# Cosine attention and a GELU feed-forward on one core: the first w_in tile takes the place of three idle matmuls, and VectorE alone sums a quad of heads in PSUM

## The chip, the cores and the metric

One core of a Trainium2 chip runs the whole program. The metric is the device time of one execution in microseconds.

## The reference

```python
q_n = q / (norm(q) + 1e-6); k_n = k / (norm(k) + 1e-6)        # q, k, v: 8 x 12 x 448 x 64, fp32
attn = softmax(q_n @ k_n.T / tau)                             # tau = 0.1
x = (attn @ v), heads side by side                            # 3584 x 768
out = gelu_exact(x @ w_in) @ w_out                            # 768 -> 2048 -> 768, fp32 result
```

## The kernel before

There are eight batches of 12 heads and 448 positions. A *quad* is four heads; a batch has three (quads 0 to 23 in all). The order of every engine's instructions is written out by hand: the program's text is the order, each engine runs its own queue in that order, and semaphores are derived from who writes and reads which tile.

**A quad.** `load_qk` brings q and k in (SP's queue). `square` (GpSimd, in the first batch ScalarE) and `reduce` (VectorE) make the squared norms `nq`; `logs` and `roots` (ScalarE: ln, then exp of half of it) and `inverses` (VectorE) make the inverse norms `rn`; `scale` (GpSimd) writes the normalised bf16 `qkb`. `transposes` turns it into `qkT`, by a transposing DMA on SP's queue or, for the first quads and quad 3, by TensorE through a PSUM bank `tp` (`copies` on VectorE takes it out). `scores` writes `st` for two of the heads' rows at a time into a pair of PSUM banks; `exps` (ScalarE) turns it into `pt`; there are seven chunks. The sum over the keys is made in one of two ways: by TensorE with a matrix of ones (`sums`, then `turned` and `inverted`), or by adding the seven `pt` chunks into `acc` (`folded` on GpSimd, `chunked` on VectorE) and then across partitions on VectorE (`turned_all`, `inverted_all`). `values` writes `o` into PSUM, `spread` and `normalise` (VectorE) write the batch's `x`.

**The feed-forward.** `first(b)` makes 16 tiles `hp` (m = 0 to 15) of x @ w_in, each of six steps kd, and their gelu `g` on ScalarE. Steps 0 and 1 need quad 0 of the batch, 2 and 3 quad 1, 4 and 5 quad 2; the weights `wi` are loaded by steps, too (`load_wi`, GpSimd's queue). The first tiles (`ahead`) do steps 0 to 3, then 4 and 5 when the last quad's x is there; the rest go tile by tile. In batches 0 and 1 ScalarE swaps its table after the gelu of tile 5, makes the norms of a coming quad, and swaps back. The second matmul (`op`, 16 steps each) is cut into single matmuls and spread as filler over the next batch's attention.

**PSUM.** Eight banks: two singles `mm0` and `mm1` that `mm_tile` hands out in turn (to `op`, `sm`, `tp`, and `hp` tiles), pairs `st0` and `st1`, and a third pair that serves `sm` and `o` in the first batch and is `st2` afterwards. In `first(b)`, `pairs` says which tiles `hp` take which pair: `{0: 1, 2: 0, 6: 1, 8: 0}` means that tiles 0 and 1 take pair 1, 2 and 3 pair 0, and so on; the others take singles.

**Around the change.** In the first batch, `spin(3)` (L453) issues three matmuls whose result nobody reads; it stands in `attention_first` behind the last scores and exponentials of quad 2 and ahead of that quad's last sums. In batch 0 the two TensorE transpositions of quad 3 stand ahead of tile m = 8:

```python
            if b == 0 and m == 8:
                for i in range(2):
                    transposes(4, i)
                    copies(4, i)
```

In batches 2 to 6, `first(b)` also sums the next batch's first quad: `chunked` reduces its first half over the seven chunks in one VectorE instruction (L268), and `folded` adds the second half chunk by chunk on GpSimd (L264).

Of the kernel before, what the change touches and what calls it, by code (L numbers as in the profile page):

```python
# [9 lines left out]
F32 = mybir.dt.float32  # L10
BF16 = mybir.dt.bfloat16
AF = mybir.ActivationFunctionType
ALU = mybir.AluOpType
# [3 lines left out]
def kernel(  # L17
# [17 lines left out]
    nc = tc.nc  # L35
    B, H, S, D = q.shape
    C = S // D
    NQ = H // 4
# [3 lines left out]
    KD = d_model // 128  # L42
    KF = d_ff // 128
    NH = d_model // 2
    NB = S // 32
# [12 lines left out]
    accp = ctx.enter_context(tc.tile_pool(name="accp", bufs=1))  # L58
# [6 lines left out]
    acc = ctx.enter_context(ExitStack())  # L65
# [27 lines left out]
    wi = wpool.tile([128, KD, d_ff], BF16, tag="wi")  # L93
# [7 lines left out]
    def mm_tile(name, shape=(128, 512), dtype=F32, aside=None):  # L101
        t = ps_mm.tile(list(shape), dtype, tag=f"mm{turn[0] if aside is None else turn[0] ^ aside}", name=name)
        if aside is None:
            turn[0] ^= 1
        return t

    def pair(i, name):
        pool = third[0] if i == 2 else ps_st
        return pool.tile([128, 2, 512], F32, tag=f"st{i}", name=name)
# [13 lines left out]
    x_t, g_t = {}, {}  # L123
# [37 lines left out]
    def reduce(u, part=slice(0, 2)):  # L161
        g, s0, s1 = units[u]
        sq = sq_t[g][:, :, s0:s1]
        n, j = place[u]
        if n not in nq_t:
            nq_t[n] = nrm.tile([128, len(groups[n]), 2, s1 - s0, C], F32, tag="nq", name=f"nq{n}")
        nq = nq_t[n][:, j]
        nc.vector.tensor_reduce(nq[:, part], sq[:, part], mybir.AxisListType.X, ALU.add)  # L168
# [54 lines left out]
    def copies(u, i):  # L223
        g, s0, s1 = units[u]
        rows = slice(64 * s0, 64 * s1)
        nc.vector.tensor_copy(qkT_t[g][rows, i], tp_t.pop((u, i))[rows])

    st_t, all_t = {}, {}
# [26 lines left out]

    acc_t = {}

    def folded(g, chunks=range(C), s=slice(0, 2)):
        for c in chunks:
            if c == 1 and g not in acc_t:  # L260
                acc_t[g] = accp.tile([128, 2, S], F32, tag="acc", name=f"acc{g}")
            if c:
                to = acc_t[g][:, s]
                nc.gpsimd.tensor_tensor(to, all_t[g][:, 0, s] if c == 1 else to, all_t[g][:, c, s], ALU.add)  # L264

    def chunked(g, s):
        acc_t[g] = accp.tile([128, 2, S], F32, tag="acc", name=f"acc{g}")
        nc.vector.tensor_reduce(acc_t[g][:, s], all_t[g][:, :, s].rearrange("p c q -> p q c"),  # L268
                                mybir.AxisListType.X, ALU.add)

    def turned_all(g):
        tr = rcp.tile([128, 2 * NB, 32], F32, tag="tr", name=f"ta{g}")
        nc.vector.transpose(tr.rearrange("p b r -> p (b r)"), acc_t.pop(g).rearrange("p s q -> p (s q)"))  # L273
        su = bank_t[g, "su"] = rcp.tile([128, 2, 2, NB], F32, tag="sa", name=f"sa{g}")
        nc.vector.tensor_reduce(su[:, 0].rearrange("p s b -> p (s b)"), tr, mybir.AxisListType.X, ALU.add)
        for j in range(4):
            o = j ^ 1
            nc.vector.tensor_reduce(su[32 * j:32 * (j + 1), 1].rearrange("p s b -> p (s b)"),
                                    su[32 * o:32 * (o + 1), 0].rearrange("p s (b n) -> p (s b) n", n=1),
                                    mybir.AxisListType.X, ALU.add)  # L280

    def inverted_all(g):
        su = bank_t.pop((g, "su"))
        s2 = rcp.tile([128, 2, NB], F32, tag="su", name=f"su{g}")
        for s in range(2):
            for h in range(2):
                nc.vector.tensor_reduce(s2[64 * s:64 * (s + 1), h],
                                        su[64 * h:64 * (h + 1), :, s].rearrange("p k b -> p b k"),
                                        mybir.AxisListType.X, ALU.add)
        rc = bank_t[g, "rc"] = rcp.tile([128, 2, NB], F32, tag="rc", name=f"rc{g}")  # L290
        nc.vector.reciprocal(rc, s2)
# [152 lines left out]
    def upto(f, n, last=None):  # L444
        last = {load_qk: NG, load_v: NV, root: len(groups), load_wi: NQ + 1, load_wo: 4}.get(f, NU)
        while done.get(f, 0) < min(n, last):
            done[f] = done.get(f, 0) + 1
            f(done[f] - 1)

    def spin(n):  # L450
        ps = ps_mm.tile([128, 512], F32, tag=f"mm{turn[0]}", name="spin")
        for _ in range(n):
            nc.tensor.matmul(ps[:, :S], lhsT=ident, rhs=blank, start=True, stop=True)  # L453

    def attention_first():
        x_t[0] = xp.tile([128, KD, S], BF16, tag="x", name="x0")
        DV, AC, GP = nc.vector, nc.scalar, nc.gpsimd
# [154 lines left out]
        scores(2, ((0, 6), (1, 6)))  # L612
        exps(2, ((0, 6), (1, 6)))
        reduce(4, Q)
        spin(3)
        sums(2, range(3, 7))
        values(2, (4,))
        logs(4)
# [169 lines left out]
    def first(b):  # L788
        sb, hf = divmod(b, 2)
        if hf == 0:  # L790
            g_t[sb] = gp.tile([128, KF, 2 * S], BF16, tag="g", name=f"g{sb}")
        nc.scalar.preload_act_table_set(GELU_SET)
        u = (b + 1) * NQ + 1
        hps = {}
        pairs = ({0: 1, 2: 0, 6: 1, 8: 0}, {2: 0, 4: 1, 6: 2, 8: 0}, {2: 2, 4: 1, 6: 0})[min(b, 2)]
        ahead = 6 if b else 5

        def mm(m, kds):
            for kd in kds:
                nc.tensor.matmul(hps[m], lhsT=wi[:, kd, m * 128:(m + 1) * 128],  # L800
                                 rhs=x_t[b][:, kd, :], start=(kd == 0), stop=(kd == KD - 1))

        def bank(m):
            if m in pairs:
                st = pair(pairs[m], f"hp{b}_{m}")
                hps[m], hps[m + 1] = st[:, 0, :S], st[:, 1, :S]
            elif m not in hps:
                hps[m] = mm_tile(f"hp{b}_{m}")[:, :S]

        for m in (0, 2, 3, 4, 5, 1) if b > 1 else range(ahead):  # L810
            bank(m)
            mm(m, range(KD - 2))
        if b == 0:
            upto(square, u + 3)
            upto(scale, u + 1)
            upto(transposes, u + 1)
            upto(load_wo, 4)
            upto(reduce, u + 3)
        else:
            late = int(b == 1)  # L820
            if b == 1:
                upto(scale, u + 1)
                upto(transposes, u + 1)
            for n in range(2, 4) if b > 1 else ():
                upto(scale, u + n)
                upto(transposes, u + n)
                upto(load_qk, (b + 1) * NQ + 6)
            upto(load_qk, (b + 1) * NQ + 5)
            upto(square, u + 3 if b == 1 else u + 4)
            if 1 < b < B - 1:  # L830
                chunked((b + 1) * NQ, 0)
                folded((b + 1) * NQ, s=slice(1, 2))
                upto(square, u + 6)
                upto(reduce, u + 4)
            upto(reduce, u + 4 - 2 * late)
            if 1 < b < B - 1:
                turned_all((b + 1) * NQ)
                inverted_all((b + 1) * NQ)
                spread((b + 1) * NQ, 0)
                spread((b + 1) * NQ, 1)  # L840
        for kds in ((KD - 2,), (KD - 1,)) if b > 1 else (range(KD - 2, KD),):
            for m in range(ahead):
                mm(m, kds)
        for m in range(KF):
# [4 lines that stand above are left out]
            if m >= ahead and (m == 0 or m - 1 not in pairs):  # L849
                for k in range(m, m + 1 + (m in pairs)):  # L850
                    bank(k)
                    mm(k, range(KD))
            nc.scalar.activation(g_t[sb][:, m, hf * S:(hf + 1) * S], hps.pop(m), AF.Gelu)  # L853
            if b <= 1 and m == 5:
                nc.scalar.preload_act_table_set(EXP_SET)
                upto(root, 6 if b == 0 else 8)
                nc.scalar.preload_act_table_set(GELU_SET)
                upto(scale, u + 2)
                upto(transposes, u + 2)
                if b == 0:  # L860
                    upto(load_qk, 2 * NQ + 1)
                else:
                    upto(square, u + 4)
                    upto(reduce, u + 4)
        if b + 1 < B:
            nc.scalar.preload_act_table_set(EXP_SET)
            if b <= 1:
                visit(b + 1, (0, 1, 2))
            upto(root, 2 * b + 6 + (b > 0))
# [63 lines left out]
```

## Time and profile before

| | |
|---|---|
| median of 3 runs | 406.95 us (406.7 to 408.2) |
| the profiled execution | 407.06 us, its span 405.3 us |
| TensorE busy | 398.9 us, 98% of the span |
| ScalarE, VectorE, GpSimd busy | 247.3, 239.0, 250.0 us |
| span of batch 0's w_in stage | 32.03 to 51.08 us |
| batch 3's w_in stage | starts at 176.2 us |

Engines are PE (TensorE matmul), PEld (its weight loads), DVE (VectorE), ACT (ScalarE), POOL (GpSimd) and SP (a queue of DMA issues). L800 is line 800 of the kernel before. `out<-in` names tiles of the program. Matmuls overlap, so the time that one costs is the distance from start to start and not its duration.

### The profile page before, as it was taken

The page shows a single profiled execution, that of the slowest core. Times are in us where ns is not written, and L with a number is a line of the kernel's source. Part 1 is how long each engine was busy: PE and PEld are TensorE (multiplying, and loading weights), DVE is VectorE, ACT ScalarE, POOL GpSimd, SP SyncE. Part 2 cuts the span into 40 slices and gives each one's busy share as a digit, 9 for nine tenths or more (in the row PEclk, how much of TensorE's full clock was granted, in tenths as well). Part 3 has the DMA queues.
Part 4 walks back from the last instruction along what each step waited for, and adds up shares of the span by engine and source line. Part 5 has one row for each costly group of instructions (what it writes and reads, how often), then busy time and mean ns, then how long its engine had stood idle before and what let it go on. Part 6 is the DMA issues. An engine that isn't in the chain of part 4 may idle for free.

```text
span 405.3 us, 8074 instructions
## 1 busy us (share of the span) xinstructions
PE 398.9 (98%) x3343; PEld 207.9 (51%) x3343; DVE 239.0 (59%) x438; ACT 247.3 (61%) x360; POOL 250.0 (62%) x160
## 2 busy tenths in 40 slices
PE   7999999999999999999999999999999999999996
PEld 3445545455555555555555555555555555455554
DVE  5787214953377976677656976758665981360021
ACT  6995686567867558656566557865656555724300
POOL 5899707075799993999829994799919940000000
PEclk9999999999999999999999999999999999999999
DMA  8999999836395714668083942769032840130033
GB/s 288 261 257 217 204 212 322 184 83 194 69 278 114 186 36 101 206 116 175 10 217 119 197 94 15 254 102 226 0 87 59 155 64 2 40 78 2 0 79 78
DMA packets 66484, 54.52 MB, mean 135 GB/s; under 512 B 38672, under 2 KB 62352, under 8 KB 66448
## 3 DMA queue, kind: packets, MB, share of 16 engines
q1 hardware_dynamic: 54464, 41.79, 40.3%
q0 software_dynamic: 11600, 11.80, 18.2%
q8 instruction: 26, 0.43, 0.4%
q10 hardware_dynamic: 384, 0.43, 0.3%
q14 instruction: 10, 0.08, 0.1%
HBM read 45.61 MB, written 11.01 MB: 140 GB/s over the span
## 4 chain that ended last, share of the span: by engine, by line
PE 91%; DMA 3%; POOL 2%; DVE 2%; issue 1%; ACT 0%; POOLq 0%
PE op L396 34%; PE hp L800 32%; PE st L242 10%; PE o L325 8%; DMA qkT<-qkb 3%; PE spin L453 2%; PE sm L311 2%; PE op L415 1%; POOL qkb L204 1%; PE sm L302 1%; POOL sq L159 1%; PE tp L221 1%; DVE nq L168 1%; DVE rn L188 0%; ACT pt L252 0%
## 5 line engine op out<-in xcount | busy, mean ns | idle before, releaser
L252 ACT ACTIVATE pt<-st 128x896 bf16<-128x896 f32 x168 | 143.1, 916 | 54.0 <-PE st L242 53.7
L396 PE MATMUL op<-wo,g 128*128 128x384 bf16 x864 | 148.9, 327 | 0.0
L800 PE MATMUL hp<-x,wi 128*128 128x448 bf16 x768 | 146.9, 353 | 0.0
L396 PEld LDWEIGHTS <-g 128*128 128x128 bf16 x864 | 81.0, 98 | 64.6 <-issue 13.9
L800 PEld LDWEIGHTS <-wi 128*128 128x128 bf16 x768 | 74.4, 98 | 71.4 <-issue 2.9
L853 ACT ACTIVATE g<-hp 128x448 bf16<-128x448 f32 x128 | 64.1, 549 | 74.0 <-PE hp L800 73.8
L204 POOL TENSOR_TENSOR qkb<-qk,rn 128x896 bf16<-128x896 f32 (+1 forms) x50 | 80.1, 1630 | 27.4 <-DVE rn L188 27.1
L400 DVE COPY ot<-op 128x384 f32<-128x384 f32 x54 | 29.3, 542 | 79.2 <-PE op L396 77.1
L264 POOL TENSOR_TENSOR acc<-acc,pt 128x896 f32<-128x896 f32 (+1 forms) x50 | 73.0, 1460 | 4.2 <-ACT pt L252 0.5
L159 POOL TENSOR_TENSOR sq<-qk 128x1792 f32<-128x1792 f32 (+1 forms) x22 | 66.5, 3038 | 14.1 <-DMA qk<-in_k_dram 14.1
L168 DVE TENSOR_REDUCE nq<-sq 128x28 f32<-128x1792 f32 (+2 forms) x30 | 48.6, 1632 | 10.3 <-POOL sq L159 7.3
L242 PE MATMUL st<-qkT 64*64 64x448 bf16 x672 | 49.5, 358 | 0.8 <-DMA qkT<-qkb 0.6
L325 PE MATMUL o<-pt,v 64*64 64x448 bf16 x672 | 37.0, 351 | 0.0
L359 DVE TENSOR_TENSOR x<-o,rs 128x448 bf16<-128x448 f32 x48 | 28.0, 610 | 13.7 <-PE o L325 12.7
L264 POOL TENSOR_TENSOR acc<-pt 128x896 f32<-128x896 bf16 (+1 forms) x10 | 14.5, 1453 | 28.6 <-ACT pt L252 28.6
L242 PEld LDWEIGHTS <-qkT 64*64 64x64 bf16 x672 | 16.8, 105 | 24.7 <-issue 18.1
L354 DVE STREAM_TRANSPOSE rs<-rc 128x448 f32<-128x448 f32 x48 | 28.6, 625 | 0.7
L268 DVE TENSOR_REDUCE acc<-pt 128x448 f32<-128x3136 bf16 x5 | 28.0, 5603 | 0.0
L325 PEld LDWEIGHTS <-v 64*64 64x64 bf16 x672 | 18.7, 107 | 14.4 <-issue 4.4
L273 DVE STREAM_TRANSPOSE ta<-acc 128x896 f32<-128x896 f32 x10 | 11.1, 1112 | 18.0 <-POOL acc L264 18.0
L333 DVE STREAM_TRANSPOSE tr<-sm 128x448 f32<-128x448 f32 x14 | 9.1, 648 | 15.1 <-PE sm L311 12.8
L186 DVE TENSOR_REDUCE se<-root 128x28 f32<-128x56 f32 (+2 forms) x18 | 4.0, 222 | 15.5 <-ACT root L180 15.3
(48 smaller groups left out, 171.1 us busy)
## 6 DMA issues: line engine op xcount, KB each, us to landing
qk<-in_q_dram SPq DMA_DIRECT2D x23, 448.0 KB, 5.3
qk<-in_k_dram SPq DMA_DIRECT2D x23, 448.0 KB, 5.8
out_dram<-ot SPq DMA_DIRECT2D x48, 192.0 KB, 3.2
v<-in_v_dram POOLq DMA_DIRECT2D x7, 672.0 KB, 6.9
wo<-in_moe_w_out_dram POOLq DMA_DIRECT2D x4, 768.0 KB, 13.9
wi<-in_moe_w_in_dram POOLq DMA_DIRECT2D x4, 512.0 KB, 14.2
out_dram<-ot SPq DMA_DIRECT2D x12, 96.0 KB, 2.2
wi<-in_moe_w_in_dram POOLq DMA_DIRECT2D x4, 256.0 KB, 14.1
```

The lines of the kernel that those rows point to most:

```text
L159: eng.tensor_tensor(sq[:, part], t[:, part], t[:, part], ALU.mult)
L168: nc.vector.tensor_reduce(nq[:, part], sq[:, part], mybir.AxisListType.X, ALU.add)
L204: eng.tensor_tensor(qkb[:, i, :, s0:s1].rearrange("p c s d -> p s c d"), t[:, i, s0:s1], rn[:, i].to_broadcast([128, s1 - s0, C, D]), ALU. ...
L242: nc.tensor.matmul(st[cols, n, :S], lhsT=qkT[rows, 1, c, cols], rhs=qkT[rows, 0, :, cols], start=True, stop=True, tile_position=(64 * s, 6 ...
L252: nc.scalar.activation(pt, st[:, :, :S], AF.Exp, scale=inv_tau)
L264: nc.gpsimd.tensor_tensor(to, all_t[g][:, 0, s] if c == 1 else to, all_t[g][:, c, s], ALU.add)
L325: nc.tensor.matmul(bank_t[g, h][cols, :S], lhsT=v_t[g][rows, s, c, :], rhs=pt_t[g, s, c][rows], start=(c == 0), stop=(c == C - 1), tile_po ...
L354: nc.vector.transpose(rs, bank_t[g, "rc"][:, h].to_broadcast([128, NB, 32]))
L396: nc.tensor.matmul(ps[:, :NH], lhsT=g_t[sb][:, kf, t * 128:(t + 1) * 128], rhs=wo[:, kf, ni * NH:(ni + 1) * NH], start=(kf == 0), stop=(kf ...
L400: nc.vector.tensor_copy(ot[:, ni * NH:(ni + 1) * NH], ps[:, :NH])
L800: nc.tensor.matmul(hps[m], lhsT=wi[:, kd, m * 128:(m + 1) * 128], rhs=x_t[b][:, kd, :], start=(kd == 0), stop=(kd == KD - 1))
L853: nc.scalar.activation(g_t[sb][:, m, hf * S:(hf + 1) * S], hps.pop(m), AF.Gelu)
```

## The change

Batch 0: the three spins are taken out. In their place stand steps 0 to 3 of tile 0 of w_in, in the single bank that the spins wrote. The later tiles take other banks: pair 1 for tiles 1-2 and 7-8, pair 0 for 3-4 and 9-10, singles for the rest. The transpositions of quad 3 still stand at m = 8, but tile 8 is then already done, as it shares a pair with tile 7.

Batches 2 to 6: the next batch's first quad is summed by VectorE alone, both halves at once, seven instructions of 128x896, into bank pair 0 in PSUM. The three squares of that stage now follow one another on GpSimd. `turned_all` transposes the accumulator in two pieces, everywhere. Batches 2 to 7: tiles 6 and 7 of w_in take single banks instead of pair 0, and tiles 8 and 9 pair 2 instead of singles.

```diff
-    def folded(g, chunks=range(C), s=slice(0, 2)):
+    def folded(g, chunks=range(C)):
         for c in chunks:
-            if c == 1 and g not in acc_t:
+            if c == 1:
                 acc_t[g] = accp.tile([128, 2, S], F32, tag="acc", name=f"acc{g}")
             if c:
-                to = acc_t[g][:, s]
-                nc.gpsimd.tensor_tensor(to, all_t[g][:, 0, s] if c == 1 else to, all_t[g][:, c, s], ALU.add)
-
-    def chunked(g, s):
-        acc_t[g] = accp.tile([128, 2, S], F32, tag="acc", name=f"acc{g}")
-        nc.vector.tensor_reduce(acc_t[g][:, s], all_t[g][:, :, s].rearrange("p c q -> p q c"),
+                nc.gpsimd.tensor_tensor(acc_t[g], all_t[g][:, 0] if c == 1 else acc_t[g], all_t[g][:, c], ALU.add)
+
+    def gathered(g, p):
+        acc_t[g] = pair(p, f"acc{g}")[:, :, :S]
+        nc.vector.tensor_reduce(acc_t[g], all_t[g][:, 0].rearrange("p s (q n) -> p s q n", n=1),
                                 mybir.AxisListType.X, ALU.add)
+        for c in range(1, C):
+            nc.vector.tensor_tensor(acc_t[g], acc_t[g], all_t[g][:, c], ALU.add)
 
     def turned_all(g):
         tr = rcp.tile([128, 2 * NB, 32], F32, tag="tr", name=f"ta{g}")
-        nc.vector.transpose(tr.rearrange("p b r -> p (b r)"), acc_t.pop(g).rearrange("p s q -> p (s q)"))
+        acc = acc_t.pop(g)
+        for s in range(2):
+            nc.vector.transpose(tr[:, s * NB:(s + 1) * NB].rearrange("p b r -> p (b r)"), acc[:, s])
...
+    early = {}
+
+    def w_in(b, t, m, kds):
+        for kd in kds:
+            nc.tensor.matmul(t, lhsT=wi[:, kd, m * 128:(m + 1) * 128], rhs=x_t[b][:, kd, :],
+                             start=(kd == 0), stop=(kd == KD - 1))
...
         reduce(4, Q)
-        spin(3)
+        early[0] = mm_tile("hp0_0")[:, :S]
+        w_in(0, early[0], 0, range(KD - 2))
         sums(2, range(3, 7))
...
-        hps = {}
-        pairs = ({0: 1, 2: 0, 6: 1, 8: 0}, {2: 0, 4: 1, 6: 2, 8: 0}, {2: 2, 4: 1, 6: 0})[min(b, 2)]
+        hps = {0: early[0]} if b == 0 else {}
+        pairs = ({1: 1, 3: 0, 7: 1, 9: 0}, {2: 0, 4: 1, 6: 2, 8: 0}, {2: 2, 4: 1, 8: 2})[min(b, 2)]
...
-        for m in (0, 2, 3, 4, 5, 1) if b > 1 else range(ahead):
+        for m in (0, 2, 3, 4, 5, 1) if b > 1 else range(b == 0, ahead):
...
-            upto(square, u + 3 if b == 1 else u + 4)
+            upto(square, u + 3 if b == 1 else u + 6)
             if 1 < b < B - 1:
-                chunked((b + 1) * NQ, 0)
-                folded((b + 1) * NQ, s=slice(1, 2))
-                upto(square, u + 6)
+                gathered((b + 1) * NQ, 0)
                 upto(reduce, u + 4)
```

More of the change, by code (lines that the diff above doesn't have):

```diff
@@ L793, in first @@
         u = (b + 1) * NQ + 1
-        hps = {}
-        pairs = ({0: 1, 2: 0, 6: 1, 8: 0}, {2: 0, 4: 1, 6: 2, 8: 0}, {2: 2, 4: 1, 6: 0})[min(b, 2)]
+        hps = {0: early[0]} if b == 0 else {}
+        pairs = ({1: 1, 3: 0, 7: 1, 9: 0}, {2: 0, 4: 1, 6: 2, 8: 0}, {2: 2, 4: 1, 8: 2})[min(b, 2)]
         ahead = 6 if b else 5
         def mm(m, kds):
-            for kd in kds:
-                nc.tensor.matmul(hps[m], lhsT=wi[:, kd, m * 128:(m + 1) * 128],
-                                 rhs=x_t[b][:, kd, :], start=(kd == 0), stop=(kd == KD - 1))
+            w_in(b, hps[m], m, kds)
         def bank(m):
```

## The prediction

> **What bounds the kernel now.** I read the page first, then the table of waits, then TensorE's timeline around the first batch's w_in stage, then ScalarE's and the load issues of the same stretch.
>
> ```profile
> PE 398.9 (98%) x3343; PEld 207.9 (51%) x3343; DVE 239.0 (59%) x438; ACT 247.3 (61%) x360; POOL 250.0 (62%) x160
> ...
> PEclk9999999999999999999999999999999999999999
> ```
>
> The table of waits (who waited for whom: us in total, times, longest) has, after the start-up, one row of a matmul's wait above 0.2 us:
>
> ```profile
> PE st L242 <- DMA qkT<-qkb: 0.6, 1, 0.6
> ```
>
> So the matrix engine sets the time. From 59.7 us to the end no matmul starts late; taking work from VectorE or GpSimd there can gain nothing, and a change gains only if it removes matmuls, and loses wherever it makes TensorE wait. TensorE's timeline from 26 to 62 us (start, duration, operation, count, idle before):
>
> ```profile
> 29.79 0.74 PE L453 MATMUL spin<-blank,ident 128*128 128x448 bf16 x3
> 30.46 0.95 PE L302 MATMUL sm<-pt,ones 128*64 128x448 bf16 x8
> 31.34 0.76 PE L325 MATMUL o<-pt,v 64*64 64x448 bf16 x12
> 32.03 9.25 PE L800 MATMUL hp<-x,wi 128*128 128x448 bf16 x48
> 41.12 0.94 PE L221 MATMUL tp<-ident,qkb 128*128 128x128 bf16 x14
> 41.90 9.24 PE L800 MATMUL hp<-x,wi 128*128 128x448 bf16 x48
> 51.08 0.76 PE L242 MATMUL st<-qkT 64*64 64x448 bf16 x12
> ...
> 58.16 0.38 PE L242 MATMUL st<-qkT 64*64 64x448 bf16 x4
> 59.16 0.57 PE L242 MATMUL st<-qkT 64*64 64x448 bf16 x8 [0.62 <-DMA qkT<-qkb]
> ```
>
> A w_in step costs (41.12 - 32.03) / 48 = 0.189 us from start to start, a spin the same. Four st matmuls cost 0.19 (x4, x8 and x12 last 0.38, 0.57, 0.76), so the next were due at 58.35 and came at 59.16: 0.81 us lost. That is the only slack of this engine after the start, and anything late before 59 us is forgiven up to 0.81 us.
>
> ScalarE in the same stretch, and GpSimd's and the load queue's answer for the second w_in load:
>
> ```profile
> 36.78 2.81 ACT L853 ACTIVATE g<-hp 128x448 bf16<-128x448 f32 x6 [3.65 <-PE hp L800]
> 39.61 1.28 ACT L855 ACT_TABLE_LOAD   x1
> 41.59 0.34 ACT L175 ACTIVATE lq<-nq,tiny 128x56 f32<-128x56 f32 x1 [0.70 <-DVE nq L168]
> 41.97 0.25 ACT L180 ACTIVATE root<-lq 128x56 f32<-128x56 f32 x1
> 42.24 1.28 ACT L857 ACT_TABLE_LOAD   x1
> 43.53 2.52 ACT L853 ACTIVATE g<-hp 128x448 bf16<-128x448 f32 x5
> ```
>
> ```profile
> 12.07 1.21 POOL L431 DMA_DIRECT2D wi<-in_moe_w_in_dram  x2
> ```
>
> ```profile
> wi<-in_moe_w_in_dram POOLq DMA_DIRECT2D x1, 512.0 KB, 18.8
> ```
>
> After the sixth gelu ScalarE swaps tables, waits for the norms (41.59) and swaps back: no gelu runs from 39.6 to 43.53. The second of the two loads issued from 12.07 starts at 12.7 and takes 18.8 us, so the weights of steps 2 and 3 are complete at 31.5 us. Before, the first matmul that needs them is at 32.03 + 0.38 = 32.4, safe by 0.9 us.
>
> **Part 1: tile 0 in place of three spins.** Removed: three spins, 3 x 0.189 = -0.57 us of TensorE. The four first steps of tile 0 are moved, not added.
>
> First new wait. The moved steps stand at 29.79. Their inputs x (batch 0, quads 0 and 1) are there: the last of these normalisations ends at 29.2. Step 2 would start at 29.79 + 2 x 0.19 = 30.17, where it needs weights that land at 31.5. With a weight load (98 ns in its rows) and the release it starts at about 31.65: a stall of 1.48 us. Behind it in TensorE's queue stand the last sums (30.46) and values of quad 2. After two steps and the 0.28 us that lay between third spin and sums, the sums start at 32.12 instead of 30.46: everything behind them is 1.66 us late. VectorE's turning of these sums (31.45, on the chain of waits) waits for them, and behind it in its queue stand the scales of the next quad. From there the chain of waits runs without slack: rn 32.56, GpSimd qkb 33.05, sq 36.34, VectorE nq 39.54, ScalarE lq 41.59, root, table, gelu at 43.53. So the seventh gelu moves from 43.53 to 45.19 and ends at 45.73 (0.54 each). GpSimd's later issues (two w_out loads at 39.46) and SP's queue (the transposing DMA at 46.50, the q and k loads behind it) move by the same 1.66.
>
> Second new wait. One tile now sits in a single bank ahead of the pairs, so the pairs hold tiles 1-2, 3-4, 7-8, 9-10; tile 5 takes the other single bank and tile 6 the first again. The two transpositions tp of quad 3 come after tile 8 instead of tile 7, and take the single banks of tiles 5 and 6. Before they took those of tiles 4 and 5, both read before the table swap. Now the second must wait for tile 6's gelu, the first one behind the swap. TensorE reaches it thus: 32.03 + 1.66 = 33.69; 16 + 10 + 24 = 50 steps, 9.46 us, to 43.15 (x of quad 2 ends at 35.06 + 1.66 = 36.7, just when step 4 wants it); the first seven transpositions 0.39 (half of 41.12 to 41.90), to 43.54. The gelu ends at 45.73, plus 0.05 for the release: the second seven start at 45.78, a stall of 2.24 us. Then 0.39 and 42 steps at 9.18 / 48: the scores that stood at 51.08 come at 54.2, 3.1 us late.
>
> What is late next. The scores of 58.35 come at 61.5. Their DMA, issued 1.66 later, lands at 59.12 + 1.66 = 60.8: in time, so the old 0.81 us is swallowed. Sum for part 1: -0.57 + 1.48 + 2.24 - 0.81 = **+2.3 us**. Later nothing gives it back: TensorE has no other wait.
>
> **Part 2: VectorE adds the quad alone (batches 2 to 6).** Removed: five VectorE reductions and thirty GpSimd adds. Added: five times seven instructions of 128x896 on VectorE. Rows:
>
> ```profile
> L268 DVE TENSOR_REDUCE acc<-pt 128x448 f32<-128x3136 bf16 x5 | 28.0, 5603 | 0.0
> L264 POOL TENSOR_TENSOR acc<-acc,pt 128x448 f32<-128x448 f32 x25 | 25.8, 1034 | 2.0
> L273 DVE STREAM_TRANSPOSE ta<-acc 128x896 f32<-128x896 f32 x10 | 11.1, 1112 | 18.0 <-POOL acc L264 18.0
> ```
>
> No row shows the new add. The nearest VectorE rows for 896 elements are the turning, 1.11, and its reduction, 1.09; bounds are 0.61 (x, 128x448, a PSUM operand) and 1.89 (GpSimd's add of this size). At 1.13 with the gap between dependent instructions: 7.9 us instead of 5.6. In batch 3 it starts at 181.15 and ends at 189.1; the reduce behind it (2.0) and the turning (now two of 0.63) follow without the 2.63 us wait for GpSimd, and the chain ends at about 196.5 against 196.7 now. The next scale waits for ScalarE's root at 197.0 anyway. The sums now sit in bank pair 0, which the next quad's values (198.1) need: read out by 192.3, 5.8 us ahead. Price taken: 0. At 1.89 per add the chain would end near 201.7, 2 us behind its x at 199.66, in five batches. GpSimd's 6.2 us per batch go, but nothing on TensorE waits for them: 0.
>
> Tile 6 of batches 2 to 7 moves from the free pair into tile 0's bank. Batch 3: the first gelu runs 182.27 to 182.82, the 37th matmul starts at 183.02, 0.20 us later; a matmul that waits for ScalarE starts 0.05 after it here (58.10 to 58.16). Taken 0; bounds 0 and, at half a gelu late, 0.3 x 6 = 1.6 us. The accumulator turned in two pieces adds 0.1 to VectorE, with 0.6 us spare before x is used (181.24 against 181.89).
>
> **A rule against the change.** The page's clock row is full throughout, and the 0.81 us pause at 58 us did not lower it. Only the first spins are slow: 0.373 us apart until 7 us, 0.189 after.
> The Trainium skill, "TensorE: Matmul & The Clock Gate", Part 1, says that TensorE falls to half clock after an idle window of about 3.4 us and needs as long to recover. By it, stalls of 1.5 and 2.2 us cost nothing more; no row here shows a pause of that length.
>
> **Sum.** The profiled execution took 407.06 (span 405.3 and 1.8 around it), 0.1 over the median 406.95 of the runs; +2.3 gives 409.4 and 409.25. I say 409.3. About 0.5% (2.0 us) is what a measurement of this kernel can tell from no change; the sum is just beyond.
>
> **The rivals.**
> Weights in time (not slower): the second w_in load is done by 30.17. Then stall one is gone, the shift is the one extra matmul, 0.19, stall two stays 2.24: -0.57 + 2.24 - 0.81 = +0.9, 407.9. Between, each 0.1 us earlier saves 0.1; below a landing at 31.2 the result is under the bound. For it: loads vary between executions. Against: eight w_in loads took 9.9 to 18.8 us and queue in order.
> The change does what it says: no new wait, -0.57, and the pause at 59.16 takes that back: 407.0. It needs the seventh gelu ahead of the swap; ScalarE's order says no.
> The clock falls in a stall: as at the start, some 14 matmuls at 0.373 for 0.189, +2.6 us: 411.9.
> VectorE or tile 6 late after all: 1.6 us or more on top, from 411.
>
> **How the numbers follow.** Both stalls 0.60 (408.6 to 410; three quarters of it beyond the bound), weights in time 0.14, no new wait 0.08, clock 0.09, VectorE or tile 6 0.07, faster for a reason I do not see 0.02. Slower: 0.45 + 0.09 + 0.07 = 0.61; faster 0.02; the rest 0.37. The range 407.4 to 411.2 holds the first two cases and part of the others.
>
> **What the profile after would show.** Right: a wait of TensorE for DMA wi of about 1.4 us at 30.2; a wait of the tp matmuls for a gelu of about 2.2 us; no wait for qkT at 61; no new TensorE waits from 130 us on; VectorE adds near 1.1 us. Wrong: no wi wait, TensorE waiting at w_in's seventh tile in batches 2 to 7, or for the turning ta at the values; a clock row below 9.

## The result, and the profile after

| | before | after |
|---|---|---|
| median of 16 runs, us | 406.83 | 410.7 |
| ratio (95% interval) | | 1.0073 (1.0046 to 1.0101) |
| profiled execution, span | 407.06, 405.3 | 411.04, 409.3 |

The kernel is slower, by 0.5 to 1.0%. Its runs form two groups: seven at 409.04 to 409.45 us with a mean TensorE clock of 0.998 to 1.0, and eight at 410.68 to 411.61 with 0.994 to 0.996. (One more, at 414.24 with 0.983, belongs to a disturbance that the kernel before shows too, at 412.56 to 414.25 with 0.983; here and below, runs with a mean clock under 0.993 are left out of such counts.) The profiled execution is of the second group.

The page after: TensorE is as busy as before, and the clock row has one dip, in the fifth slice.

```profile
PE 399.6 (98%) x3340; PEld 207.7 (51%) x3340; DVE 250.2 (61%) x478; ACT 246.6 (60%) x360; POOL 219.3 (54%) x130
...
PEclk9999899999999999999999999999999999999999
```

The table of waits after. The row of scores waiting for the transposing DMA is gone, and two new rows of TensorE stand in its place:

```profile
PE tp L221 <- ACT g L860: 2.0, 1, 2.0
...
PE hp L462 <- DMA wi<-in_moe_w_in_dram: 1.7, 1, 1.7
...
PE st L242 <- ACT pt L252: 0.2, 1, 0.2
```

TensorE's timeline after, the same stretch as before:

```profile
29.40 0.55 PE L462 MATMUL hp<-x,wi 128*128 128x448 bf16 x2
31.63 0.54 PE L462 MATMUL hp<-x,wi 128*128 128x448 bf16 x2 [1.68 <-DMA wi<-in_moe_w_in_dram]
32.10 0.95 PE L305 MATMUL sm<-pt,ones 128*64 128x448 bf16 x8
...
33.67 9.67 PE L462 MATMUL hp<-x,wi 128*128 128x448 bf16 x50
43.19 0.55 PE L221 MATMUL tp<-ident,qkb 128*128 128x128 bf16 x7
45.77 0.55 PE L221 MATMUL tp<-ident,qkb 128*128 128x128 bf16 x7 [2.03 <-ACT g L860]
46.16 9.79 PE L462 MATMUL hp<-x,wi 128*128 128x448 bf16 x42
55.88 0.76 PE L242 MATMUL st<-qkT 64*64 64x448 bf16 x12
...
62.96 0.76 PE L242 MATMUL st<-qkT 64*64 64x448 bf16 x12
```

Two steps of tile 0, a pause until the weights land (31.50 in this execution), then sums, w_in steps, half of the transpositions, a pause for a gelu, the other half. Then something that no wait explains: 42 steps take 9.79 us where 48 took 9.24 before. Nine of them, from 47.02 on, start 0.373 us apart. ScalarE's timeline shows the gelu that the second pause ends with, behind the table load:

```profile
43.24 0.34 ACT L175 ACTIVATE lq<-nq,tiny 128x56 f32<-128x56 f32 x1 [1.41 <-DVE nq L168]
43.61 0.25 ACT L180 ACTIVATE root<-lq 128x56 f32<-128x56 f32 x1
43.88 1.28 ACT L864 ACT_TABLE_LOAD   x1
45.17 1.42 ACT L860 ACTIVATE g<-hp 128x448 bf16<-128x448 f32 x3
```

And the table by stretches, of three windows around the slow steps (columns: busy us of each engine, granted clock, DMA share, GB/s):

```profile
core 0: us, PE busy (x) PEld busy (x) DVE busy (x) ACT busy (x) POOL busy (x), PEclk, DMA share, GB/s
43.40:46.80 3.40, 1.37 (x18) 0.97 (x15) 1.69 (x4) 3.13 (x6) 2.01 (x2) 1.00 1.26 202
46.80:50.20 3.40, 3.40 (x11) 1.35 (x10) 0.18 (x1) 0.00 (x0) 3.40 (x3) 0.50 1.31 204
50.20:53.60 3.40, 3.40 (x20) 1.75 (x18) 0.00 (x0) 2.06 (x4) 1.21 (x1) 1.00 1.30 197
```

The clock is halved from 46.80 to 50.21, 3.41 us, just behind a stretch of that length in which TensorE worked 1.37 us of 3.40. That costs nine steps 0.184 us each, 1.66 us, and is the distance between the two groups (411.0 and 409.3).

VectorE in batch 3, its rows for the new sum:

```profile
185.34 1.09 DVE L267 TENSOR_REDUCE acc<-pt 128x896 f32<-128x896 bf16 x1
186.46 6.98 DVE L270 TENSOR_TENSOR acc<-acc,pt 128x896 f32<-128x896 f32 x6
193.35 2.01 DVE L168 TENSOR_REDUCE nq<-sq 128x28 f32<-128x1792 f32 x1
195.27 1.17 DVE L276 STREAM_TRANSPOSE ta<-acc 128x448 f32<-128x448 f32 x2
```

The sum takes 8.1 us, 1.10 per add; what follows it in the queue ends at 200.7, exactly as far into the batch as before (196.7 plus the 4.0 us by which everything is late).

### The profile page after: what moved, and what is told of

It is laid out like the page before. It is cut to its first block, busy times and chain, and to the rows that moved or that the text cites. A ratio compares the mean times of both kernels' runs of the same rounds, so it can differ in the third digit from the quotient of the medians.

```text
span 409.3 us, 8055 instructions
## 1 busy us (share of the span) xinstructions
PE 399.6 (98%) x3340; PEld 207.7 (51%) x3340; DVE 250.2 (61%) x478; ACT 246.6 (60%) x360; POOL 219.3 (54%) x130
## 4 chain that ended last, share of the span: by engine, by line
PE 88%; DMA 5%; POOL 3%; issue 2%; DVE 1%; ACT 1%; POOLq 0%
PE op L399 35%; PE hp L462 34%; PE st L242 8%; PE o L328 7%; DMA wi<-in_moe_w_in_dram 5%; PE sm L314 2%; POOL qkb L204 1%; PE op L418 1%; POOL sq L159 1%; DVE nq L168 0%; POOL wi L434 0%; POOL v L144 0%; ACT L864 0%; PE sm L305 0%; DVE tr L336 0%
## 5 line engine op out<-in xcount | busy, mean ns | idle before, releaser
L462 PE MATMUL hp<-x,wi 128*128 128x448 bf16 x768 | 148.9, 355 | 1.7 <-DMA wi<-in_moe_w_in_dram 1.7
L263 POOL TENSOR_TENSOR acc<-acc,pt 128x896 f32<-128x896 f32 x25 | 47.1, 1886 | 2.4 <-ACT pt L252 0.6
L270 DVE TENSOR_TENSOR acc<-acc,pt 128x896 f32<-128x896 f32 x30 | 33.0, 1099 | 2.0
L263 POOL TENSOR_TENSOR acc<-pt 128x896 f32<-128x896 bf16 x5 | 9.4, 1880 | 28.4 <-ACT pt L252 28.4
L276 DVE STREAM_TRANSPOSE ta<-acc 128x448 f32<-128x448 f32 x20 | 11.7, 624 | 7.0 <-POOL acc L263 7.0
```

Of the source, the lines that this page charges most:

```text
L263: nc.gpsimd.tensor_tensor(acc_t[g], all_t[g][:, 0] if c == 1 else acc_t[g], all_t[g][:, c], ALU.add)
L270: nc.vector.tensor_tensor(acc_t[g], acc_t[g], all_t[g][:, c], ALU.add)
L462: nc.tensor.matmul(t, lhsT=wi[:, kd, m * 128:(m + 1) * 128], rhs=x_t[b][:, kd, :], start=(kd == 0), stop=(kd == KD - 1))
```

## The experiments

**Which part costs.** The first kernel has the changed sum and banks of batches 2 to 7, and batch 0 as before.

```diff
-        early[0] = mm_tile("hp0_0")[:, :S]
-        w_in(0, early[0], 0, range(KD - 2))
+        spin(3)
...
-        pairs = ({1: 1, 3: 0, 7: 1, 9: 0}, ...
+        pairs = ({0: 1, 2: 0, 6: 1, 8: 0}, ...
```

> Part 2 alone: batch 0 as in the kernel before (three spins, old banks); VectorE sums the quad in PSUM, tiles 6 to 9 of batches 2 to 7 in the changed banks. Theory (all of the loss arises in batch 0): no difference that can be measured, 406.8 within 0.3 us, no TensorE wait after 60 us. Rival (VectorE or tile 6 late): 1 us or more above the kernel before, with waits of hp or o matmuls in batches 2 to 7.

Measured: 407.02 us, ratio 0.9991 (0.9975 to 1.0008). In its TensorE timeline the old wait is back, and by the table of waits no hp, o or op matmul waits for an engine or a DMA:

```profile
57.77 0.38 PE L242 MATMUL st<-qkT 64*64 64x448 bf16 x4
59.13 0.57 PE L242 MATMUL st<-qkT 64*64 64x448 bf16 x8 [0.97 <-ACT pt L252]
```

(The row names ScalarE, one of whose exponentials ended at the same moment; the weight load ahead of these matmuls had waited for the transposing DMA, which landed at 59.09.) The second kernel has the other half: batch 0 as in the changed kernel, the rest as before.

> Part 1 alone: batch 0 as in the changed kernel, batches 2 to 6 summed as before. Theory: as the changed kernel, 409.2 where the clock stays full, 410.9 where it is halved once for 3.4 us behind the second stall. Rival (part 2 has a share): 0.5 us or more away from the changed kernel.

Measured: 411.13 us, ratio 1.0105 (1.0060 to 1.0151); of five undisturbed runs one at 409.3 and four at 410.82 to 411.43. Part 2 alone costs nothing that shows, and part 1 alone costs as much as the whole change: the loss is in batch 0.

**The second stall, and the first alone.** The changed kernel with one more pair:

```diff
-        pairs = ({1: 1, 3: 0, 7: 1, 9: 0}, ...
+        pairs = ({1: 1, 3: 0, 5: 2, 7: 1, 9: 0}, ...
```

> The changed kernel, with tiles 5 and 6 of batch 0 in the third bank pair, so that the two transpositions of quad 3 take banks that are read before the table swap. Theory: the 2.2 us stall is gone and with it the halved clock; the stall for the weights stays, and its shift of 1.66 us now shows at the scores that wait for the transposing DMA (1.5 us in place of 0.8): 408.5, clock full in nearly every execution. Rival (the weight stall is hidden in that old wait): 407.0. Rival (the first stall is what lowers the clock): the clock still falls in half of the executions, 409 or more as a median.

Measured: 407.36 us, ratio 1.0032 (0.9996 to 1.0067); in the nine undisturbed runs the clock is 0.999 or 1.0 (three of the twelve, at 411.52 to 412.80 with 0.983 to 0.988, lie below the 0.993 given above). Its TensorE timeline:

```profile
30.53 0.55 PE L462 MATMUL hp<-x,wi 128*128 128x448 bf16 x2
31.89 0.54 PE L462 MATMUL hp<-x,wi 128*128 128x448 bf16 x2 [0.81 <-DMA wi<-in_moe_w_in_dram]
...
43.44 0.94 PE L221 MATMUL tp<-ident,qkb 128*128 128x128 bf16 x14
...
59.34 0.76 PE L242 MATMUL st<-qkT 64*64 64x448 bf16 x12
```

The fourteen transpositions run through: the bank was the cause of the second stall. But 408.5 was wrong, by the landing of the transposing DMA. It was issued at 48.40, 1.9 us later than before, and landed at 58.73, not at 60.8. So a stall for weights alone is nearly hidden in the old wait, and the rival's 407.0 was the better number. (This execution reached the place of the spins at 30.53 and paused 0.98 us, where the changed kernel paused 1.85.)

**The first stall taken away.** The changed kernel with only the two steps whose weights are there:

```diff
-        w_in(0, early[0], 0, range(KD - 2))
+        w_in(0, early[0], 0, range(2))
...
-            mm(m, range(KD - 2))
+            mm(m, range(2 if b == 0 and m == 0 else 0, KD - 2))
```

> The changed kernel, with only steps 0 and 1 of tile 0 in place of the spins (their weights have landed); steps 2 and 3 follow in the old place. Theory: no wait for the weights; the transposition still waits for tile 6's gelu, 1.9 us; sum -0.6 + 1.9 - 0.8 = +0.5, 407.3 where the clock stays full, 409 where it is halved. Rival (only the weight stall costs): 406.8 or less.

Measured: 407.7 us, ratio 1.0013 (0.9995 to 1.0031). Nine undisturbed runs, 407.26 to 408.68, all with a clock of 1.0. No wait for weights, and of the transpositions:

```profile
41.51 0.55 PE L221 MATMUL tp<-ident,qkb 128*128 128x128 bf16 x7
43.75 0.55 PE L221 MATMUL tp<-ident,qkb 128*128 128x128 bf16 x7 [1.69 <-ACT g L860]
```

The expected 407.3 is the lower end of these. No half clock came with this stall, which by the row is 0.34 us shorter than that of the changed kernel. By the medians of the undisturbed runs, the first stall alone (407.25) and the second alone (407.67) cost 0.25 and 0.67 us over the kernel before on the same chip (407.00); neither is clear of noise, as both intervals hold 1. Both together cost 2.5 even in the group without a half clock (409.33 against 406.83): the old wait forgives once.

**Both taken away.** The two edits together:

> The changed kernel with both waits taken away: steps 0 and 1 alone in place of the spins, tiles 5 and 6 in the third pair. Theory: TensorE never waits in the w_in stage of batch 0 and the clock stays full; it then waits for the transposing DMA of quad 4, whose landing (58.3 to 59.1 in every run so far, 0.4 to 1.0 behind the last w_out load) does not follow TensorE: 406.9 within 0.3, the same as the kernel before, the three spins saved for nothing. Rival (the landing follows the issue): 0.6 us faster, 406.3.

Measured: 406.93 us, ratio 1.0005 (0.9982 to 1.0028). TensorE runs through the w_in stage and then waits for the same DMA, which landed at 59.37:

```profile
58.10 0.38 PE L242 MATMUL st<-qkT 64*64 64x448 bf16 x4
59.41 0.57 PE L242 MATMUL st<-qkT 64*64 64x448 bf16 x8 [0.93 <-DMA qkT<-qkb]
```

So the three spins are worth nothing here: what they free is waited for at 59 us.

**The clock.** The changed kernel with the second stall filled with work that nobody reads:

```diff
                 for i in range(2):
+                    if i:
+                        ps = pair(2, "busy")
+                        for _ in range(11):
+                            nc.tensor.matmul(ps[:, 0, :S], lhsT=ident, rhs=blank, start=True, stop=True)
                     transposes(4, i)
```

> The changed kernel with eleven idle matmuls into the third pair, 2.1 us, between the two transposition groups of quad 3, so that TensorE works through the second stall. Theory (the stall lowers the clock): 409.3 in every execution and no half clock behind it; the share near 411 is gone. Rival (the half clock has another cause): still two groups, 409.3 and 411.

Measured: 409.61 us, five runs from 409.34 to 409.99, ratio 1.0059 (1.0043 to 1.0074), all with a clock of 0.999 or 1.0. TensorE's timeline and the table by stretches:

```profile
43.17 0.55 PE L221 MATMUL tp<-ident,qkb 128*128 128x128 bf16 x7
43.56 2.25 PE L857 MATMUL busy<-blank,ident 128*128 128x448 bf16 x11
45.76 0.55 PE L221 MATMUL tp<-ident,qkb 128*128 128x128 bf16 x7
46.15 8.11 PE L462 MATMUL hp<-x,wi 128*128 128x448 bf16 x42
```

```profile
43.40:46.80 3.40, 3.40 (x28) 2.00 (x26) 1.70 (x4) 3.12 (x6) 2.02 (x2) 1.00 1.26 202
46.80:50.20 3.40, 3.40 (x20) 1.76 (x19) 0.17 (x1) 1.42 (x3) 3.40 (x3) 1.00 1.32 205
```

The second transpositions start where they did (45.76 against 45.77), the 42 steps behind them take 8.11 us instead of 9.79, and the group at 411 is gone. With the changed kernel's seven runs of fifteen without a fall, five such runs in a row would come by luck about once in 45 times. The pause is the cause of the half clock.

Why the same kernel falls in one execution and not in another, the traces show in part. In all eleven of them the granted clock changes only on a grid: from where it first went full, at 4.57 to 7.86 us, it stayed full for a whole number of stretches of 3.413 us (12 in the changed kernel and with part 1 alone, 16 and 18 in two kernels below, 117 or 118 where nothing fell before the last matmuls). Stretches of this grid, of a kernel below with a pause of 2.46 us and no fall, of another with 2.08 us and a fall, and of the end of the kernel with the first stall taken away:

```profile
60.18:63.59 3.41, 2.85 (x22) 1.30 (x21) 0.56 (x1) 2.33 (x3) 2.81 (x1) 1.00 1.36 136
63.59:67.01 3.41, 1.51 (x12) 0.80 (x15) 0.01 (x1) 0.00 (x0) 0.37 (x1) 1.00 1.21 208
...
58.03:61.45 3.41, 1.41 (x14) 0.73 (x15) 0.04 (x1) 1.86 (x3) 0.00 (x0) 1.00 1.07 248
61.45:64.86 3.41, 3.41 (x18) 1.23 (x16) 0.00 (x0) 0.75 (x1) 0.91 (x1) 0.50 1.30 176
...
400.72:404.13 3.41, 1.45 (x22) 1.23 (x19) 0.71 (x2) 0.00 (x0) 0.00 (x0) 1.00 0.49 114
404.13:407.54 3.41, 0.00 (x0) 0.00 (x0) 0.00 (x0) 0.00 (x0) 0.00 (x0) 1.00 0.01 3
```

In the eleven traces, every stretch of the grid in which TensorE was busy 1.41 us or less is followed by half clock, and none with 1.45 us or more is. So a pause lowers the clock when enough of it falls into one stretch, and the 2.46 us pause was cut by a stretch's end at 63.59. This was found in the traces afterwards, and no run was made to test it; one execution of each kernel was traced, so for the other runs it is an inference.

**What the transposing DMA waits for.** In all the runs above it lands at 58.3 to 59.4, 0.4 to 1.0 us behind the last w_out load, whether issued at 46.1 or 48.4. So the second pair of w_out loads was issued later, in the kernel with both stalls taken away and in the kernel before:

```diff
-            upto(load_wo, 4)
...
                 if b == 0:
+                    upto(load_wo, 4)
                     upto(load_qk, 2 * NQ + 1)
```

> The kernel with both waits taken away, and the second pair of w_out loads issued behind quad 4's scale, about 7 us later, so that quad 4's transposing DMA has the queues to itself. Theory (that DMA lands behind the w_out loads in front of it): it lands before TensorE asks for it, no wait at 58 us, 405.5 to 406.1, faster than both kernels. Rival (all loads together bound it): 406.9. Rival (the w_out half comes late): op matmuls wait near 64 us, over 407.

> The kernel before with the second pair of w_out loads issued behind quad 4's scale alone. Theory: the old pause of 0.81 us for the transposing DMA is gone, 406.1. Rivals as for the mended kernel: 406.9, or over 407 with op matmuls waiting near 64 us.

Measured: 410.82 us, ratio 1.0083 (1.0065 to 1.0101), and 410.77, ratio 1.0074 (1.0051 to 1.0096). The DMA did land early, at 55.66 and 56.02, and no score waited for it. But the last w_out load landed at 65.72 and 65.46, and op stood for it. The row of the mended kernel's table of waits:

```profile
PE op L399 <- DMA wo<-in_moe_w_out_dram: 3.3, 1, 3.3
```

Here too the clock falls: in the profile of the first from 66.14 on, right behind the pause, and by the mean clock (0.995 or 0.996) in five of six runs of the one and four of six of the other. A third try moved the last load alone (`upto(load_wo, 3)` in the old place):

> The kernel with both waits taken away, and the last w_out load alone issued behind quad 4's scale (at about 46.5 instead of 40.4), the third in its old place. Theory (the landings follow the order of issue at a rate that the loads share): the transposing DMA lands near 57.5, in time for its scores, and the last w_out half near 62, when op's ninth step asks for it: 406.0 to 406.5, a little under the kernel before. Rival (the last load comes late again): a wait of op of 1 us or more near 63 us, 407.5 or more, the clock halved in some executions.

Measured: 410.32 us over twelve runs, ratio 1.0068 (1.0034 to 1.0101). In its profile the transposing DMA, issued at 46.38, landed at 60.00 and the scores waited for it 2.08 us by the row; the last w_out load landed at 62.92. The theory that landings follow the order of issue fails on this run. Of eight undisturbed runs three were at 406.52 to 407.05, and four had a half clock. What exactly decides that landing stays open; that these loads share a rate was not shown. Each of the three orders tried only chose which load TensorE waited for. No version beat the kernel before.

## Why the prediction was right, point by point

The forecast of 409.3 is the group of runs without a half clock, 409.04 to 409.45; the median lies 1.4 us above it, inside the range, on the side forecast. Both stalls came as forecast. That the median is still in the range is in part luck: it lies above the 408.6 to 410 of the case with chance 0.60, because of a half clock that this case did not have, and at the price that the prediction gave to that (411.9) it would have lain outside.

- *First stall.* Step 2 was due at 31.65 and came at 31.63; the sums 32.12, came 32.10. It was sized 1.48 and was 1.85, only because this execution reached the place 0.39 us earlier; the landing fixed its end. That it agrees to 0.02 us is luck: over the eleven traces that load landed between 31.17 and 31.97. None was near the 30.17 that the rival "weights in time" needed.
- *Second stall.* Transpositions at 43.15 and 45.78, came 43.19 and 45.77. The step "the second must wait for tile 6's gelu, the first one behind the swap" holds; another bank for tile 6 removes it.
- *What is late next.* "Lands at 59.12 + 1.66 = 60.8" was wrong: 58.59. A landing time was moved with its issue, while other loads were in flight. It did no harm, since the scores came at 61.5 or later; it did harm in the expectation for tiles 5 and 6 in the third pair.
- *Part 2.* Price 0: shown, 0.9991. The add was put at 1.13 with its gap and took 1.10 without it, 8.1 us in all against 7.9. Tile 6 kept its 0.20 us behind the first gelu in every batch.
- *The clock.* This is the term that was mis-sized, in chance and in price. "The clock falls in a stall" had 0.09 and 2.6 us; it happened in eight of fifteen runs and cost 1.66, as one stretch of 3.41 us at half rate. The price was taken from the start-up, where the clock is low for longer (the spins from 1.95 to 7.07 us). "A clock row below 9" stands in the prediction's own list of signs of being wrong, and the fifth slice of the row after shows 8.

The Trainium skill, "TensorE: Matmul & The Clock Gate", Part 1, gives the gate a free-running window of about 3.4 us, and the half clock here lasts 3.41. Its condition, an idle window, is not what these runs show: before the fall TensorE had worked 1.37 us of 3.40. The measurement decides. That the window runs free agrees with the grid of 3.413 us above, which starts at another time in each trace.

## What to carry to other kernels

Idle matmuls in front of a dependence can only be replaced without a new wait by work whose inputs are there at that time: look up when the weights land, step by step, not whether they land before the old first use. Moving a tile by one place turns the rotation of the single banks; list who reads each bank last, above all across a table swap on ScalarE. Where one wait already stands late in a stage, stalls in front of it are forgiven up to its length once, so two that cost little alone (0.25 and 0.67 us here) can cost 2.5 us together.

## What was not expected of the hardware

A pause of TensorE shorter than the clock's stretch already halves the clock. By the idle column of TensorE's rows: no fall in nine runs at 1.69 us; falls in eight of fifteen and in four of five at 2.03; in four of eight at 2.08; in four of six at 2.46; in five of six at 3.32. Each fall ahead of the last matmuls lasts 3.41 us in the profiles, 1.66 us lost where steps of 0.189 run back to back. What counts in the eleven traces is TensorE's busy time in a stretch of a 3.413 us grid: 1.41 us or less was followed by half clock, 1.45 or more was not.

A transposing DMA issued up to 1.9 us later landed up to 0.8 us earlier (46.50 to 59.12 before, 48.10 to 58.32 with batch 0 alone changed), while w_out loads of another queue were in flight. The last of these, issued 1.6 us later as well, landed 1.3 us earlier (58.62 and 57.32).
